# The second expert block's first product by seven block products (Strassen's 2x2 scheme), tokens in halves

## The chip, the core and the metric

The kernel runs on one core of a Trainium2 chip. A core has a matrix engine (TensorE, PE in the rows), a vector engine (VectorE, DVE), a scalar engine (ScalarE, ACT), a general engine (GpSimd, POOL) and a queue engine (SyncE, SP) that issues the transfers here. Each takes its own instructions in order and waits on semaphores for the others. TensorE reads SBUF and writes PSUM (eight banks of 128x512 float32); the others move results back to SBUF. The metric is the device time of one execution in microseconds (us), as a median of several.

## The reference, cut to what matters

```python
# attn_out: causal linear attention with decay, B=2, H=8, S=768, D=64 -> x of 1536 tokens x 512
# part one (1536 tokens, 512 -> 2048 -> 512)
h = x @ w_in
g = h * clip(h + 3, 0, 6) / 6
x = g @ w_out
# part two: 8 experts, each 512 -> 1024 -> 512, all tokens through all experts
logits = x @ w_gate;  P = exp(logits - logits.max())
for _ in range(8):
    P /= P.sum(1, keepdims=True) + 1e-9
    P /= P.sum(0, keepdims=True) + 1e-9
    P *= N / E
for e in range(8):
    h = maximum(x @ w1[e], 0)          # "first product"
    out += P[:, e:e+1] * (h @ w2[e])   # "second product"
```

The inputs w_in and w_out come as float64; everything else is float32.

## The kernel before

Every large product is made in three float32r matmuls of 128 rows: each operand is split into a rounded part hi and a rest lo, and hi x hi, hi x lo and lo x hi are summed in PSUM. ScalarE makes a hi (a copy), VectorE the lo behind it (a subtraction).

Attention takes the first 80 us or so. Then one list of steps, `steps`, runs: 48 steps of part one (three token blocks of 512, the 16 tiles of 128 hidden features in groups of 4, 6, 6), then 192 steps of part two (8 experts x 3 token blocks x 8 tiles of 128 hidden features). A step has a `stage_a` (12 matmuls at L312: one tile of the hidden h for 512 tokens, over 4 slices of the 512 inputs, in PSUM tag "s0") and a `stage_b` (12 matmuls at L348: what this tile adds to four accumulators of 128x512 in tags "s1" and "r"). `stage_a` of step s+2 is issued ahead of `stage_b` of step s (`LOOK` = 2), so that the hidden tile is evicted (L327 hi with ReLU, L328 lo) two steps before it is needed. `finish` takes the accumulators to `o` after the last tile of a group: L380 multiplies by the gate P and adds.

The weights of both parts come through one queue of loads and splits (`load_w`, `splitting`, L163 and L165 in part two), 13 slots deep, worked off by `pump` between steps. Each weight of part two is loaded once.

The gate hangs on the steps by a table, `put`: logits of a block as three times eight float32r matmuls (L407), transposes (L415), then from the third step of part two on one call of `gate_cols` a step: a small matmul (L453, tile gc) that sums columns over all tokens, and eight short VectorE instructions (L457 to L447) that normalise P by columns and by rows; the next call's matmul needs their result.

```python
    put(2 * (NSF + 3), gate_exp)
    for i in range(NITER):
        put(2 * (NSF + 4 + i), gate_cols, i == NITER - 1)
```

Of the kernel before, what the change touches and what calls it, by code (L numbers as in the profile page):

```python
# [18 lines left out]
P = 128  # L19
# [12 lines left out]
NLD = E * F2T  # L32
NW = 8
NX = 5
# [13 lines left out]
def kernel(  # L48
# [15 lines left out]

    ps_s = ctx.enter_context(tc.tile_pool(name="ps_s", bufs=2, space=PSUM))
    const = ctx.enter_context(tc.tile_pool(name="const", bufs=1))
    xp = ctx.enter_context(tc.tile_pool(name="xp", bufs=NBLK))
    wp = ctx.enter_context(tc.tile_pool(name="wp", bufs=NW))
    sk = ctx.enter_context(tc.tile_pool(name="sk", bufs=2))
    sp = ctx.enter_context(tc.tile_pool(name="sp", bufs=3))  # L70

    wg_raw = const.tile([P, KT, E], F32, name="wg_raw")
    lg = const.tile([P, NTT, E], F32, name="lg")
# [6 lines left out]
    wkeys = [("f", i) for i in range(F1T)] + [("e", i) for i in range(NLD)]  # L80
# [3 lines left out]
    raw_next = iter([u for u in units if u[0] == "f" or u[2] == 0])  # L84
    state_ = {"started": 0, "done": 0, "step": -1}

    def load_w():
        unit = next(raw_next, None)
        if unit is None:
            return  # L90
        kind, i, part = unit
        t = sp.tile([P, 2 * BLK], U32, tag="raw", name="raw")
        if kind == "f":
            nc.sync.dma_start(out=t, in_=wf_in[i, :, part * BLK:(part + 1) * BLK].bitcast(U32))
            raw_t[unit] = t
        else:
            nc.sync.dma_start(out=t, in_=we_in[i].bitcast(U32))
            for j in range(2):
                raw_t[kind, i, j] = t[:, j * BLK:(j + 1) * BLK]

    def slot_free():
        n = state_["started"] // 2
        if n < NW:
            return True
        if n < NW + NX:
            return "x" in pools
        return last_use[wkeys[n - NW - NX]] <= state_["step"]

    def splitting():
# [8 lines left out]
        for kind, i, part in units:  # L118
# [8 lines left out]
            if part == 0:  # L127
                pool = pools["x" if index[kind, i] % (NW + NX) >= NW else "w"]
                hi = pool.tile([P, 2 * BLK], F32R, tag="whi", name="whi")
                lo = pool.tile([P, 2 * BLK], F32R, tag="wlo", name="wlo")  # L130
                w_t[kind, i] = (hi, lo)
            r = slice(part * BLK, (part + 1) * BLK)
            if kind == "f":

                word = t.rearrange("p (n t) -> p n t", t=2)
                lw, hw = word[:, :, 0], word[:, :, 1]
                top = t.bitcast(U16).rearrange("p (n t) -> p n t", t=4)[:, :, 3]
                w = sp.tile([P, BLK], U32, tag="w", name="w", bufs=2)
                nc.vector.tensor_scalar(out=w, in0=lw, scalar1=29, scalar2=None, op0=ALU.logical_shift_right)  # L139
                yield True  # L140
                nc.vector.scalar_tensor_tensor(  # L141
                    out=w, in0=hw, scalar=0x80000000, in1=w, op0=ALU.bitwise_and, op1=ALU.bitwise_or
                )
                yield True
                nc.vector.tensor_scalar(out=top, in0=top, scalar1=0x7FFF, scalar2=None, op0=ALU.bitwise_and)  # L145
                nc.scalar.activation(out=top, in_=top, func=AF.Relu, bias=ebias, scale=1.0)  # L146
                yield True
                if tail:
                    low()
                    yield True  # L150
                nc.vector.scalar_tensor_tensor(  # L151
                    out=w, in0=hw, scalar=3, in1=w, op0=ALU.logical_shift_left, op1=ALU.bitwise_or
                )
                load_w()
                t = w.bitcast(F32)
                nc.scalar.activation(out=hi[:, r], in_=t, func=AF.Copy)
                tail.append((lo[:, r], t, hi[:, r]))
                yield True
            else:
                t = t.bitcast(F32)  # L160
                if tail:
                    low()
                nc.scalar.activation(out=hi[:, r], in_=t, func=AF.Copy)  # L163
                yield True
                nc.vector.tensor_tensor(out=lo[:, r], in0=t, in1=f32(hi[:, r]), op=ALU.subtract)  # L165
                if part:
                    load_w()
                state_["done"] += 1
                yield True
# [8 lines left out]
    def rate(s):  # L178

        most = 2  # L180
        for n, k in enumerate(wkeys):
            left = 2 * n + 2 - state_["done"]
            if left > 0 and first_use[k] <= s + 12:
                most = max(most, -(-left * (5 if k[0] == "f" else 2) // max(1, first_use[k] - LOOK - s)))
# [7 lines left out]
    x_t, x2_t = {}, {}  # L192

    def x_tiles(name):
        hi = xp.tile([P, KT, BLK], F32R, tag="xhi", name=name + "hi")
        lo = xp.tile([P, KT, BLK], F32R, tag="xlo", name=name + "lo")
# [3 lines left out]
    at = ctx.enter_context(ExitStack())  # L200
    at1 = at.enter_context(tc.tile_pool(name="at1", bufs=1))
    at2 = at.enter_context(tc.tile_pool(name="at2", bufs=2))
# [66 lines left out]
    def attend(n):  # L269
# [17 lines left out]
        if at_ == 0:  # L287
            x_t[bl] = x_tiles("x")
# [11 lines left out]
    steps += [("e", b, e * F2T + f, f, F2T, e) for e in range(E) for b in range(NBLK) for f in range(F2T)]  # L300
    g_t, acc_b, mo = {}, {}, {}

    def stage_a(s):
        kind, b, wi, f, nf, part = steps[s]
        whi, wlo = weights((kind, wi))
        xhi, xlo = (x_t if kind == "f" else x2_t)[b]
# [9 lines left out]
        if kind == "f":  # L316
            t = sp.tile([P, BLK], F32, tag="t", name="t", bufs=1)
            nc.scalar.activation(out=t, in_=h, func=AF.Relu, bias=three, scale=1.0)  # L318
            pump(1)
            nc.vector.scalar_tensor_tensor(  # L320
                out=t, in0=t, scalar=6.0, in1=h, op0=ALU.min, op1=ALU.mult
            )
            nc.scalar.activation(out=hi, in_=t, func=AF.Copy)  # L323
            pump(1)
            nc.vector.tensor_tensor(out=lo, in0=t, in1=f32(hi), op=ALU.subtract)  # L325
        else:
            nc.scalar.activation(out=hi, in_=h, func=AF.Relu)  # L327
            nc.vector.scalar_tensor_tensor(  # L328
                out=lo, in0=h, scalar=0.0, in1=f32(hi), op0=ALU.max, op1=ALU.subtract
            )  # L330
        g_t[s] = (hi, lo)

    def stage_b(s):
# [6 lines left out]
        for i in range(4):  # L340
            cs = slice(i * P, (i + 1) * P)
            ws = slice(BLK + i * P, BLK + (i + 1) * P)
            if kind == "f":
                ops = [(whi[:, ws], ghi), (whi[:, ws], glo), (wlo[:, ws], ghi)]
            else:
                ops = [(ghi[:, cs], whi[:, BLK:]), (ghi[:, cs], wlo[:, BLK:]), (glo[:, cs], whi[:, BLK:])]
            for j, (l, r) in enumerate(ops):
# [3 lines left out]
            if f == nf - 1:  # L351
                finish(kind, b, part, i)

    def finish(kind, b, part, i):
        o = mo["o"]
        tt = b * 4 + i
        if kind == "f" and part == 0:
            nc.scalar.activation(out=o[:, tt], in_=acc_b[i], func=AF.Copy)  # L358
# [267 lines left out]
```

## Time and profile before

| | |
|---|---|
| time, median of 3 runs | 1411.91 us (1411.49 to 1413.43) |
| the profiled execution: its time, its span in the trace | 1412.86 us, 1411.0 us |
| TensorE busy | 1390.6 us, 99% of the span |
| VectorE busy | 498.6 us, 35% |
| ScalarE busy | 341.1 us, 24% |
| transfers | 68.90 MB, 49 GB/s on average |

A matmul's own record overlaps the next one's, so the busy time of TensorE says that it was never without work, and not how long one matmul holds it: that is the distance from start to start. For VectorE and ScalarE the duration of a record is read as it stands; two that are independent of one another overlap a little.

### The profile page before, as it was taken

The page shows a single profiled execution, that of the slowest core. Times are in us where ns is not written, and L with a number is a line of the kernel's source. Part 1 is how long each engine was busy: PE and PEld are TensorE (multiplying, and loading weights), DVE is VectorE, ACT ScalarE, POOL GpSimd, SP SyncE. Part 2 cuts the span into 40 slices and gives each one's busy share as a digit, 9 for nine tenths or more (in the row PEclk, how much of TensorE's full clock was granted, in tenths as well). Part 3 has the DMA queues.
Part 4 walks back from the last instruction along what each step waited for, and adds up shares of the span by engine and source line. Part 5 has one row for each costly group of instructions (what it writes and reads, how often), then busy time and mean ns, then how long its engine had stood idle before and what let it go on. Part 6 is the DMA issues. An engine that isn't in the chain of part 4 may idle for free.

```text
span 1411.0 us, 14967 instructions
## 1 busy us (share of the span) xinstructions
PE 1390.6 (99%) x6379; PEld 1136.4 (81%) x6379; DVE 498.6 (35%) x820; ACT 341.1 (24%) x548; POOL 26.9 (2%) x26
## 2 busy tenths in 40 slices
PE   7899999999999999999999999999999999999998
PEld 6678788888888888888888888888888888888887
DVE  5876767554442321222123222222221232121211
ACT  3565545443211211111122111111121111111110
POOL 3300000000000000000000000000000000000000
PEclk9999999999999999999999999999999999999999
DMA  8622212121100110011011001200110011000000
GB/s 328 218 82 82 75 60 75 46 61 44 45 16 15 45 45 15 31 45 45 0 45 46 30 1 45 60 16 15 45 45 16 31 45 45 0 0 1 30 30 30
DMA packets 20370, 68.90 MB, mean 49 GB/s; under 512 B 2512, under 2 KB 2512, under 8 KB 20304
## 3 DMA queue, kind: packets, MB, share of 16 engines
q1 hardware_dynamic: 20304, 67.95, 14.7%
q8 instruction: 50, 0.82, 0.3%
q14 instruction: 16, 0.13, 0.0%
HBM read 64.79 MB, written 3.15 MB: 48 GB/s over the span
## 4 chain that ended last, share of the span: by engine, by line
PE 92%; DVE 4%; ACT 2%; DMA 1%; issue 1%; SPq 0%; ACTq 0%
PE acc L348 46%; PE h L312 45%; ACT raw L146 1%; DMA raw<-in_wf 1%; DVE w L151 1%; DVE raw L145 1%; DVE a L251 1%; DVE w L141 0%; PE l L407 0%; DVE w L139 0%; DVE xlo L292 0%; DVE t L320 0%; ACT t L318 0%; DVE glo L325 0%; ACT ghi L323 0%
## 5 line engine op out<-in xcount | busy, mean ns | idle before, releaser
L328 DVE SCALAR_TENSOR_TENSOR glo<-h,ghi 128x512 fp32r<-128x512 f32 x192 | 132.8, 692 | 751.9 <-ACT ghi L327 751.8
L327 ACT ACTIVATE ghi<-h 128x512 fp32r<-128x512 f32 x192 | 114.7, 597 | 866.7 <-PE h L312 866.7
L312 PE MATMUL h<-x2hi,whi 128*128 128x512 f32 x768 | 302.8, 394 | 0.0
L348 PE MATMUL acc<-whi,ghi 128*128 128x512 f32 x768 | 302.1, 393 | 0.0
L348 PE MATMUL acc<-wlo,ghi 128*128 128x512 f32 x768 | 302.1, 393 | 0.0
L312 PE MATMUL h<-x2hi,wlo 128*128 128x512 f32 x768 | 301.9, 393 | 0.0
L348 PE MATMUL acc<-whi,glo 128*128 128x512 f32 x768 | 301.6, 393 | 0.0
L312 PE MATMUL h<-x2lo,whi 128*128 128x512 f32 x768 | 300.1, 391 | 0.0
L348 PEld LDWEIGHTS acc<-whi,glo 128*128 128x128 f32 x768 | 144.7, 188 | 32.8
L348 PEld LDWEIGHTS acc<-wlo,ghi 128*128 128x128 f32 x768 | 144.7, 188 | 32.5
L312 PEld LDWEIGHTS h<-x2lo,whi 128*128 128x128 f32 x768 | 144.7, 188 | 32.5
L348 PEld LDWEIGHTS acc<-whi,ghi 128*128 128x128 f32 x768 | 144.3, 188 | 32.9
L312 PEld LDWEIGHTS h<-x2hi,wlo 128*128 128x128 f32 x768 | 144.2, 188 | 32.9
L312 PEld LDWEIGHTS h<-x2hi,whi 128*128 128x128 f32 x768 | 144.3, 188 | 31.1
L165 DVE TENSOR_TENSOR wlo<-raw,whi 128x512 fp32r<-128x512 f32 x128 | 87.4, 683 | 14.8 <-ACT whi L163 14.8
L163 ACT ACTIVATE whi<-raw 128x512 fp32r<-128x512 f32 x128 | 79.9, 624 | 15.2 <-PE acc L348 15.2
L312 PE MATMUL h<-xhi,whi 128*128 128x512 f32 x192 | 75.5, 393 | 0.8 <-DVE t L320 0.8
L348 PE MATMUL acc<-ghi,whi 128*128 128x512 f32 x192 | 75.6, 394 | 0.5 <-ACT o L358 0.5
L348 PE MATMUL acc<-ghi,wlo 128*128 128x512 f32 x192 | 75.6, 394 | 0.0
L348 PE MATMUL acc<-glo,whi 128*128 128x512 f32 x192 | 75.4, 393 | 0.0
L312 PE MATMUL h<-xhi,wlo 128*128 128x512 f32 x192 | 75.2, 392 | 0.0
L312 PE MATMUL h<-xlo,whi 128*128 128x512 f32 x192 | 75.2, 392 | 0.0
(83 smaller groups left out, 841.6 us busy)
## 6 DMA issues: line engine op xcount, KB each, us to landing
raw<-in_we SPq DMA_DIRECT2D x64, 512.0 KB, 3.5
raw<-in_wf SPq DMA_DIRECT2D x32, 512.0 KB, 3.6
qk<-in_qk SPq DMA_DIRECT2D x12, 512.0 KB, 5.0
kv<-in_kv SPq DMA_DIRECT2D x12, 512.0 KB, 5.8
out<-o SPq DMA_DIRECT2D x12, 256.0 KB, 2.1
tq<-in_tq SPq DMA_DIRECT2D x5, 256.0 KB, 5.4
dmask<-in_dmask SPq DMA_DIRECT2D x2, 256.0 KB, 4.1
gk<-in_gk SPq DMA_DIRECT2D x1, 24.0 KB, 7.0
```

Of the source, the lines that this page charges most:

```text
L145: nc.vector.tensor_scalar(out=top, in0=top, scalar1=0x7FFF, scalar2=None, op0=ALU.bitwise_and)
L146: nc.scalar.activation(out=top, in_=top, func=AF.Relu, bias=ebias, scale=1.0)
L151: nc.vector.scalar_tensor_tensor(out=w, in0=hw, scalar=3, in1=w, op0=ALU.logical_shift_left, op1=ALU.bitwise_or)
L163: nc.scalar.activation(out=hi[:, r], in_=t, func=AF.Copy)
L165: nc.vector.tensor_tensor(out=lo[:, r], in0=t, in1=f32(hi[:, r]), op=ALU.subtract)
L251: nc.vector.tensor_tensor(out=a, in0=t[j], in1=dmask[:, j], op=ALU.mult)
L312: nc.tensor.matmul(h, w[:, ks], x[:, k], start=(n == 0), stop=(n == 3 * KT - 1))
L327: nc.scalar.activation(out=hi, in_=h, func=AF.Relu)
L328: nc.vector.scalar_tensor_tensor(out=lo, in0=h, scalar=0.0, in1=f32(hi), op0=ALU.max, op1=ALU.subtract)
L348: nc.tensor.matmul(acc_b[i], l, r, start=(f == 0 and j == 0), stop=(f == nf - 1 and j == 2))
```

## The change

Part two is taken out of the step list. Tokens are handled in two halves of 768 (`NU` = 2, `UT` = 768), each half in two parts of 384 (`SB`). For one pair of hidden tiles (256 features; 32 pairs a half, 64 in all) the first product is a 2x2 block product: two halves of the 512 inputs, two hidden tiles, two token parts. Winograd's form of Strassen's scheme makes it in seven block products instead of eight. Each block product (`product`) is six matmuls of 384 columns: two input slices, three terms each. The sums of token blocks are made once a half (`x_forms`: four VectorE sums and seven splits of 128x768), the sums of weight blocks for every pair (`w1_forms`: four sums of 256 columns, splits of 512, 256, 512 and 512), and the products are put together in `pair` by five VectorE additions of 384 columns and two ScalarE copies, before four ReLU splits (`relu_parts`). The second product (`outputs`) keeps its matmuls of 512 columns, 36 a pair, and is spread between the block products of the next two pairs: an iteration `it` issues pairs 2it and 2it+1 and the second product of pairs 2it-2 and 2it-1. The first iteration has no second product to spread, and at the turn to the second half of the tokens (it = 16) the second product is issued in one piece ahead of the pairs, together with that half's `x_forms`. As each weight is used for either half, it is loaded and split twice. The gate's calls follow one another from the third slot of the first iteration on, one a slot (a slot is one block product), its logits as plain float32 matmuls of 32 output columns. In part one, `finish` writes the tiles y2 of 768 tokens, weights have 10 slots in place of 13, and in its last six steps the first `x_forms` and `w1_forms` are made. `stage_a`, `stage_b`, `finish` and `splitting` lose their branches for part two.

```diff
...
+    def parts(hi, lo, t):
+        nc.scalar.activation(out=hi, in_=t, func=AF.Copy)
+        nc.vector.tensor_tensor(out=lo, in0=t, in1=f32(hi), op=ALU.subtract)
+
+    def w1_forms(i):
+        r = raw1.pop(i)
...
+        parts(hi[:, A11:A12 + 1], lo[:, A11:A12 + 1], r[:, 0].rearrange("p (k c) -> p k c", k=2))
+        yield True
+        nc.vector.tensor_tensor(out=t[:, S1 - S1], in0=a21, in1=a22, op=ALU.add)
+        yield True
+        nc.vector.tensor_tensor(out=t[:, S3 - S1], in0=a11, in1=a21, op=ALU.subtract)
+        yield True
+        nc.vector.tensor_tensor(out=t[:, S2 - S1], in0=t[:, S1 - S1], in1=a11, op=ALU.subtract)
+        parts(hi[:, A22], lo[:, A22], a22)
+        yield True
+        nc.vector.tensor_tensor(out=t[:, S4 - S1], in0=a12, in1=t[:, S2 - S1], op=ALU.subtract)
+        load_pair(i + 2, 0)
+        yield True
+        for n in range(2):
+            parts(hi[:, S1 + 2 * n:S3 + 1 + 2 * n], lo[:, S1 + 2 * n:S3 + 1 + 2 * n], t[:, 2 * n:2 * n + 2])
+            yield True
...
+    def product(i, bank, w, x, start, stop):
+        whi, wlo = w1_t[i]
+        xhi, xlo = xf[x]
+        n = 0
+        for k in range(2):
+            ks = slice(k * P, (k + 1) * P)
+            for l, r in ((whi, xhi), (whi, xlo), (wlo, xhi)):
+                nc.tensor.matmul(
+                    bank[:, 0:SB], l[:, w, ks], r[:, k],
+                    start=(start and n == 0), stop=(stop and n == 5), skip_group_check=True,
+                )
+                n += 1
+
+    def relu_parts(i, f, j, t):
...
+        nc.scalar.activation(out=hi, in_=t, func=AF.Relu)
+        nc.vector.scalar_tensor_tensor(out=lo, in0=t, scalar=0.0, in1=f32(hi), op0=ALU.max, op1=ALU.subtract)
+        q_t[i, f, j] = (hi, lo)
+
+    def pair(i):
...
+        b1 = bank("s0")
+        product(i, b1, A11, B11, True, True)
+        yield
+        p1 = tmp("p1")
+        nc.scalar.activation(out=p1, in_=b1[:, 0:SB], func=AF.Copy)
+        b2 = bank("s0")
+        product(i, b2, S2, T2, True, True)
+        yield
+        u2 = tmp("u2")
+        add(u2, b2[:, 0:SB], p1)
+        b3 = bank("s1")
+        product(i, b3, S1, T1, True, True)
+        yield
+        p5 = tmp("p5")
+        nc.scalar.activation(out=p5, in_=b3[:, 0:SB], func=AF.Copy)
+        b4 = bank("r")
+        product(i, b4, S3, T3, True, True)
+        yield
+        u3 = tmp("u3")
+        add(u3, b4[:, 0:SB], u2)
+        product(i, b1, A12, B21, False, True)
+        yield
+        relu_parts(i, 0, 0, b1[:, 0:SB])
+        product(i, b3, S4, B22, False, True)
+        yield
+        add(p1, b3[:, 0:SB], u2)
+        add(p5, u3, p5)
+        relu_parts(i, 0, 1, p1)
+        product(i, b4, A22, T4, False, True)
+        yield
+        relu_parts(i, 1, 1, p5)
+        add(u3, b4[:, 0:SB], u2)
+        relu_parts(i, 1, 0, u3)
+        yield
+
+    def outputs(n):
...
+            acc = ps_s.tile([P, BLK], F32, tag="y", name="acc")
+            for f in range(4):
...
+                for k, (l, r) in enumerate(((ghi, whi), (ghi, wlo), (glo, whi))):
+                    nc.tensor.matmul(
+                        acc, l[:, cs], r[:, f % 2], start=(f == 0 and k == 0), stop=(f == 3 and k == 2)
+                    )
...
+        for it in range(NIT // 2 + 1):
+            outs = outputs(it - 1) if it else iter(())
+            chunks = 4 * TU if it else 0
...
+            if turn:
+                forming = x_forms(2 * it // NPR)
+                for n in range(chunks):
+                    next(outs)
+                    if n % 3 == 0:
+                        next(forming, None)
+                drain(forming)
+                chunks = 0
+            done = slot = 0
+            for n, i in enumerate(range(2 * it, min(2 * it + 2, NIT))):
+                job = itertools.chain(*jobs[n])
+                for _ in pair(i):
+                    slot += 1
+                    while done * 16 < chunks * slot:
+                        next(outs)
+                        done += 1
+                    for _ in range(2 if it else 1):
+                        next(job, None)
+                    if 2 < slot:
+                        fn = next(gate, None)
+                        if fn:
+                            fn()
+                drain(job)
+            drain(outs)
```

Three places show how instructions stand now. First, TensorE's list at one of the gate's small matmuls: before, in the first steps of part two.

```order
L348 MATMUL acc<-wlo,ghi 128x512
L348 MATMUL acc<-whi,glo 128x512
L453 MATMUL gc<-pm,ones 128x96
L312 MATMUL h<-x2hi,whi 128x512
L312 MATMUL h<-x2lo,whi 128x512
```

And after, in the second pair of the first iteration.

```order
L551 MATMUL h<-xl,w1hi 128x384
L551 MATMUL h<-xh,w1lo 128x384
L425 MATMUL gc<-pm,ones 128x96
L551 MATMUL h<-xh,w1hi 128x384
L551 MATMUL h<-xl,w1hi 128x384
```

Between two such small matmuls there stood 24 matmuls of 512 columns before; now there are the six of 384 columns of one block product.

Second, VectorE's list in that place (second pair of the first iteration): one turn of the gate's chain, what stands ahead of it and behind it. Here s and w1lo belong to the weight forms of the next pair, u_2929 and u_2883 to this pair's sums.

```order
L483 TENSOR_TENSOR s<-s,raw_2666 128x256
L467 TENSOR_TENSOR w1lo<-raw_2666,w1hi 128x256
L429 TENSOR_REDUCE c<-gc 128x8
L432 TENSOR_SCALAR c<-c 128x8
L435 RECIPROCAL c<-c 128x8
L436 TENSOR_TENSOR pm<-pm,c 128x96
L416 TENSOR_REDUCE r<-pm 128x12
L417 TENSOR_SCALAR r<-r 128x12
L418 RECIPROCAL r<-r 128x12
L419 TENSOR_TENSOR pm<-pm,r 128x96
L569 TENSOR_TENSOR u_2929<-h,u_2883 128x384
L486 TENSOR_TENSOR s<-raw_2666,s 128x256
```

Seven such turns stand in the first iteration, one between any two block products of its second pair; before, two instructions of the step stood between two turns, and a turn fell on every step.

Third, VectorE's list within one pair of a middle iteration (o is the eviction of the second product, gl the ReLU split, p and u the sums of block products).

```order
L467 TENSOR_TENSOR w1lo<-raw_4219,w1hi 128x256
L569 TENSOR_TENSOR u_4481<-h,p_4465 128x384
L640 SCALAR_TENSOR_TENSOR o<-acc,pm,o 128x512
L486 TENSOR_TENSOR s<-raw_4219,s 128x256
L467 TENSOR_TENSOR w1lo<-s,w1hi 128x512 x2
L467 TENSOR_TENSOR w2lo<-raw_4258,w2hi 128x512
L569 TENSOR_TENSOR u_4521<-h,u_4481 128x384
L640 SCALAR_TENSOR_TENSOR o<-acc,pm,o 128x512
L467 TENSOR_TENSOR w2lo<-raw_4258,w2hi 128x512
L562 SCALAR_TENSOR_TENSOR gl<-h,gh 128x384
```

A pair has 22 VectorE instructions: five of 512 columns for weight splits, three of 512 for evictions, nine of 384 and five of 256. Before, a step had one of 512 for the hidden tile, and evictions and weight splits in bursts.

## Rows read from the trace of the kernel before

**Rows 1.** The page's first part: busy time and share of the span, instructions.

```profile
PE 1390.6 (99%) x6379; PEld 1136.4 (81%) x6379; DVE 498.6 (35%) x820; ACT 341.1 (24%) x548; POOL 26.9 (2%) x26
```

**Rows 2.** The page's chain that ended last, by engine and by line.

```profile
PE 92%; DVE 4%; ACT 2%; DMA 1%; issue 1%; SPq 0%; ACTq 0%
PE acc L348 46%; PE h L312 45%; ACT raw L146 1%; DMA raw<-in_wf 1%; DVE w L151 1%; DVE raw L145 1%; DVE a L251 1%; DVE w L141 0%; PE l L407 0%; DVE w L139 0%; DVE xlo L292 0%; DVE t L320 0%; ACT t L318 0%; DVE glo L325 0%; ACT ghi L323 0%
```

**Rows 3.** Windows: part one's end, and part two (busy us and records of each engine).

```profile
core 0: us, PE busy (x) PEld busy (x) DVE busy (x) ACT busy (x) POOL busy (x), PEclk, DMA share, GB/s
200.00:320.00 120.00, 120.00 (x524) 97.58 (x523) 73.56 (x121) 56.49 (x85) 0.50 (x2) 1.00 0.21 66
800.00:1000.00 200.00, 200.00 (x869) 163.22 (x868) 48.19 (x73) 32.67 (x57) 0.00 (x0) 1.00 0.09 27
```

**Rows 4.** Groups by line and form: TensorE's matmuls of part two.

```profile
L312 PE MATMUL h<-x2hi,whi 128*128 128x512 f32 x768 | 302.8, 394 | 0.0
L348 PE MATMUL acc<-whi,ghi 128*128 128x512 f32 x768 | 302.1, 393 | 0.0
```

**Rows 5.** Timelines of TensorE and of its weight loads (PEld) around one gc.

```profile
370.65 0.35 PE L453 MATMUL gc<-pm,ones 128*128 128x96 f32 x2
370.79 0.48 PE L312 MATMUL h<-x2hi,whi 128*128 128x512 f32 x1
371.11 0.39 PE L312 MATMUL h<-x2lo,whi 128*128 128x512 f32 x1
...
370.76 0.19 PEld L312 LDWEIGHTS h<-x2hi,whi 128*128 128x128 f32 x1
370.88 0.19 PEld L312 LDWEIGHTS h<-x2lo,whi 128*128 128x128 f32 x1
```

**Rows 6.** Groups by line and form: VectorE, long and short instructions.

```profile
L165 DVE TENSOR_TENSOR wlo<-raw,whi 128x512 fp32r<-128x512 f32 x128 | 87.4, 683 | 14.8 <-ACT whi L163 14.8
L380 DVE SCALAR_TENSOR_TENSOR o<-acc,pm,o 128x512 f32<-128x512 f32 x84 | 57.2, 743 | 4.9 <-PE acc L348 4.9
L378 DVE TENSOR_SCALAR o<-acc,pm 128x512 f32<-128x512 f32 x8 | 5.4, 745 | 0.0
L447 DVE TENSOR_TENSOR pm<-pm,r 128x96 f32<-128x96 f32 x8 | 2.1, 258 | 0.3
```

**Rows 7.** Timeline of VectorE: four evictions in a row.

```profile
437.46 2.72 DVE L378 TENSOR_SCALAR o<-acc,pm 128x512 f32<-128x512 f32 x4
```

**Rows 8.** Timeline of VectorE: one turn of the gate's chain.

```profile
405.50 0.26 DVE L457 TENSOR_REDUCE c<-gc 128x8 f32<-128x96 f32 x1 [1.66 <-PE gc L453]
...
407.28 0.26 DVE L447 TENSOR_TENSOR pm<-pm,r 128x96 f32<-128x96 f32 x1
```

**Rows 9.** Groups by line and form: ScalarE, a long and a short one.

```profile
L163 ACT ACTIVATE whi<-raw 128x512 fp32r<-128x512 f32 x128 | 79.9, 624 | 15.2 <-PE acc L348 15.2
L439 ACT ACTIVATE pm<-lg,nm 128x96 f32<-128x96 f32 x1 | 0.4, 376 | 2.2 <-DVE nm L438 2.2
```

**Rows 10.** Timeline of TensorE in attention: plain float32 matmuls, full and half width.

```profile
23.56 1.06 PE L261 MATMUL r<-kv,ks 128*128 128x128 f32 x8
...
25.63 1.09 PE L276 MATMUL y<-a,kv 128*64 128x128 f32 x16
```

**Rows 11.** Groups: the gate's work on TensorE.

```profile
L407 PE MATMUL l<-x2lo,wg 128*128 128x512 f32 x12 | 4.8, 396 | 0.0
L453 PE MATMUL gc<-pm,ones 128*128 128x96 f32 x16 | 2.8, 258 | 0.0
L415 PE MATMUL lt<-ones,l 16*128 16x16 f32 x12 | 1.3, 214 | 0.0
```

**Rows 12.** Windows in attention: TensorE's busy time and its granted clock (PEclk).

```profile
8.00:11.45 3.45, 1.62 (x26) 1.50 (x28) 0.42 (x1) 0.00 (x0) 1.04 (x1) 1.00 1.04 411
11.45:14.87 3.42, 3.42 (x24) 2.87 (x20) 1.16 (x3) 0.97 (x2) 0.29 (x1) 0.50 1.03 407
43.10:46.50 3.40, 1.78 (x24) 1.28 (x22) 2.30 (x3) 1.50 (x4) 1.75 (x2) 1.00 1.00 359
```

**Rows 13.** The page's issues of transfers: part two's weights.

```profile
raw<-in_we SPq DMA_DIRECT2D x64, 512.0 KB, 3.5
```

More of the change, by code (lines that the diff above doesn't have):

```diff
@@ L92, in load_w @@
         t = sp.tile([P, 2 * BLK], U32, tag="raw", name="raw")
[L93 to L99, printed above, removed]
+        nc.sync.dma_start(out=t, in_=wf_in[i, :, part * BLK:(part + 1) * BLK].bitcast(U32))
+        raw_t[unit] = t
+    LATE = F1T - GROUPS[-1]
     def slot_free():
@@ L299 @@
         steps += [("f", b, f0 + f, f, n, g) for b in range(NBLK) for f in range(n)]
-    steps += [("e", b, e * F2T + f, f, F2T, e) for e in range(E) for b in range(NBLK) for f in range(F2T)]
-    g_t, acc_b, mo = {}, {}, {}
+    g_t, acc_b, mo, y2 = {}, {}, {}, {}
     def stage_a(s):
@@ L402, in logits @@
-    def logits(b):
-        t = ps_s.tile([P, BLK], F32, tag="y", name="l")
-        n = 0
-        for k in range(KT):
-            for x in x2_t[b]:
-                nc.tensor.matmul(t, mo["wg"][:, k], x[:, k], start=(n == 0), stop=(n == 2 * KT - 1))
-                n += 1
-        mo["l"] = l = sp.tile([P, BLK], F32, tag="t", name="l", bufs=1)
-        nc.scalar.activation(out=l[0:2 * E], in_=t[0:2 * E], func=AF.Copy)
-    def logits_to_rows(b):
-        t = ps_s.tile([P, 4, 2 * E], F32, tag="y", name="lt")
-        for i in range(4):
+                finish(b, part, i)
@@ L493, with drain @@
+    def drain(it):
+        for _ in it:
+            pass
     last_use, first_use = {}, {}
@@ new lines @@
+        for i in range(2):
+            load_pair(i, 1)
+        gate = [lambda n=n, f=f: f(n) for n in (2, 3) for f in (logits, logits_to_rows)]
+        gate += [gate_max, gate_max2, gate_exp]
+        gate += [lambda i=i: gate_cols(i == NITER - 1) for i in range(NITER)]
+        gate = iter(gate)
+        for it in range(NIT // 2 + 1):
+            outs = outputs(it - 1) if it else iter(())
+            chunks = 4 * TU if it else 0
+            jobs = []
+            for i in (2 * it, 2 * it + 1):
+                if i < NIT:
+                    jobs.append([w1_forms(i + 1)] if i + 1 < NIT else [])
+                    jobs[-1].append(w2_parts(i))
+            turn = it and (2 * it) % NPR == 0 and 2 * it < NIT
+            if turn:
[3 more added lines that the diff above has]
+                    if n % 3 == 0:
+                        next(forming, None)
+                drain(forming)
+                chunks = 0
[15 more added lines that the diff above has]
+            drain(outs)
+            for i in (2 * it - 2, 2 * it - 1):
+                w2_t.pop(i, None)
```

426 lines of the change are left out of this document (256 added, 170 removed).

## The prediction

> **What bounds the kernel now.** The page's first part comes first: TensorE has a record running for 99% of the span, VectorE for 35% [rows 1]. The chain of waits says that this is no coincidence: 92% of the path to the end is TensorE, and nearly all of that the two matmul lines of the steps [rows 2]. The windows then show where: from 200 us on TensorE never idles, at full granted clock, with VectorE busy for 48 of 200 us in part two [rows 3]. So the time of part two is its number of matmuls times their distance, and other engines count only where they keep TensorE waiting.
>
> The distance is not the 394 ns of a record, which overlaps its neighbour [rows 4]. 869 records in 200 us are one per 0.2302 us [rows 3]. Each product of part two has three groups of 768 such matmuls, of which one stands for either in [rows 4]: 2304 of them, 2304 x 0.2302 = 530.4 us for each product.
>
> **The first product: 2304 matmuls of 512 columns become 2688 of 384.** (64 pairs x 7 block products x 6.) The columns fall by an eighth, the number grows by a sixth, so all hangs on what one of 384 costs, which no row shows. Bounds: if all of 0.2302 us goes with the columns, 0.75 x 0.2302 = 0.1727 us. If only the streaming does, one column a cycle at the 2.4 GHz that the full granted clock is, then 128 columns less save 0.0533 us: 0.1769 us. I take 0.1745, near the middle, as nothing in the rows favours either. 2688 x 0.1745 = 469.1 us, **-61.3 us** (-66.2 to -54.9).
>
> The Trainium skill (TensorE: Matmul & The Clock Gate, "Back-to-back issue gap") puts the distance at the columns over 2.4 GHz plus about 2.5 ns. That would be 216 ns for 512 columns where the windows give 230 [rows 3], so the trace disagrees; for 384 columns it would be 162.5 ns, and this term -93.6 us by it.
>
> Can the weight load, which must run ahead of every matmul, be the limit? Behind a gc, whose own matmuls are too short to hide loads, two float32r loads of 128x128 start 0.12 us apart (370.76, 370.88), and the next only with the matmul at 371.11 [rows 5]. So a load needs about 0.12 us and lies beside 0.1745.
>
> **The second product** keeps 2304 matmuls of 512 columns: 0 us.
>
> **Does VectorE keep up in a middle iteration?** A pair has 42 matmuls of 384 columns and 36 of 512: 7.33 + 8.29 = 15.6 us of TensorE. VectorE's sizes are new; I draw a line through 258 ns for 96 columns and 683 for 512 [rows 6]: 421 ns for 256, 552 for 384, 945 for 768. A pair has five weight splits of 512 (3.42), three evictions of 743 ns (2.23) [rows 6], five sums or splits of 256 (2.10), and nine of 384 (4.97): 12.7 us. Records overlap a little: four evictions in a row take 2.72 us [rows 7], 0.68 each against 0.745 [rows 6], so 0.065 less for each of 22 behind another: 11.3 us. It fits with 2.9 to 4.3 us to spare. The order gives the waits room as well: TensorE adds to b1, b3 and b4 again two slots (about 4 us) after VectorE or ScalarE could read them, and the two banks of acc are turned over every 5 us. ScalarE has 12 instructions a pair, at 624 ns for 512 columns and less for 384 [rows 9] some 7 us. I put small waits at **+2 us** over the 60 interleaved pairs (0 to +18).
>
> Weights are loaded twice: two transfers of 512 KB a pair, which land in 3.5 us [rows 13], for 15.6 us of work, issued two pairs ahead. The six output transfers at the turn stand ahead of loads in SP's queue, but those loads are for two pairs later. Hidden: 0. Part one's last six steps take on 11 instructions of 768 columns (10.4 us), eight of `w1_forms` (4.2 us) and their own work (some 8 us) on VectorE, within 33 us of matmuls; VectorE was busy 74 of 120 us there [rows 3]. Hidden: 0, but for the wait named below.
>
> **The first iteration** has no second product to cover it, and the gate in it. TensorE has 84 matmuls, 14.7 us. VectorE, with sizes as above less the overlap: its first pair has six instructions of 512 (3.7), five of 256 (1.8), nine of 384 (4.4) and four short ones of the gate (0.9), 10.8 us. Some 1.5 to 2 us come on top, since three of the four gl stand right behind the ScalarE instruction that they need (about 0.55 us for 384 columns between the two sizes of [rows 9]), so 13.0. Its second pair has 9.3 us of the same, the part around the exponential (1.2 us) and seven turns of the chain. A turn takes 2.04 us from the first instruction's start to the last one's end [rows 8]: 14.3 us. That is 24.8 us. Between two turns goes the round to TensorE's gc and back, about 0.65 us, mostly behind the 0.9 us of other VectorE work that stands there. With 3.5 us for what isn't covered and for splits behind ScalarE, 28.3. TensorE is tied to it: each gc stands ahead of the next block product and waits for the turn before. The block product (1.05 us) runs while the next turn does, and then TensorE waits. So the iteration takes 13.0 + 28.3 = 41.3 us where its matmuls take 14.7: **+26.6 us** (+15, if waits are nil and the gate's instructions slip under the first pair, to +33).
>
> **The turn to the second half.** The second product in one piece is 72 matmuls, 16.6 us, and covers `x_forms` (11 x 0.88 = 9.7 us) and six evictions (4.1). Pairs 32 and 33 then run without cover: VectorE has 9.3 us a pair and about 1.6 behind ScalarE, 10.9, twice 21.8 us, against 14.7: **+7.1 us** (+3 to +12).
>
> **The gate outside that iteration.** Before, it cost TensorE 24 logits matmuls (5.5 us), eight gc that push the next matmul back by 0.23 us each (370.65 to 371.11 is two distances [rows 5]), 1.8 us, and 12 transposes [rows 11] of about 0.1 us: 8.5 us. Now two of the four logits stand in part one. A plain float32 record of 128 columns takes about 0.11 us at full width (8 in 0.9 us), and 16 records of half width took no longer than 8 of full width [rows 10]: different column groups of the array ran side by side. Four of 384 columns on 32 output columns each are then 0.7 us (2.7 if not side by side). With six transposes (1.3), one gc (0.2) and one wait of 1.6 us, where the first logits need the last of eight half-size additions of `finish` just issued, that is 4.5 us: **-4.0 us** (-4 to 0).
>
> **The sum** is made against the profiled execution: its span of 1411.0 us, with 1.9 us around it; it is 1.0 us above the median, and only differences are carried over. -61.3 + 2 + 26.6 + 7.1 - 4.0 = -29.6. From 1411.9: 1382.3, **1382 us**.
>
> **Rivals.**
> *VectorE becomes the bound in the middle (slower).* If records don't overlap (12.7 us) and seven hand-overs between VectorE and ScalarE in a pair cost 0.6 us each, it needs 16.9 us a pair against 15.6. 60 pairs x 1.3 = +78 in place of +2, 1458 us. It turns slower than before above 16.1 us a pair. For: the gl at a pair's end come in a chain, sum, ScalarE, VectorE, three times. Against: 4 us of room, and hand-overs cover one another when two splits are under way.
> *The weight load is the bound (slower).* Then 384 columns cost what 512 do: 2688 x 0.2302 = 618.8, 150 us more than I put in, 1532 us. The change loses from 0.1855 us a matmul on. The two starts 0.12 us apart speak against it.
> *A cheap opening.* If the gate's instructions slip into waits that VectorE has anyway, the first iteration costs 12 us less: 1370 us.
> *Small waits.* 0.3 us in each interleaved pair, as each block product now carries a wait of its own where a step had few: +18 in place of +2, 1398 us.
> *No cost beyond streaming.* If the 17 ns that 512 columns take beyond 213 went away for shorter matmuls, 384 would take 0.160 us: -39 more, 1343 us. Against: every matmul of 512 columns in the windows carries that cost. By the rule of the Trainium skill cited above it would be 1350.
> *The clock falls in the first iteration.* TensorE would have work there for little over a third of the time. In attention the clock stayed at 2.4 GHz with 1.78 of 3.40 us busy, but after 1.62 of 3.45 us busy came a stretch at 1.2 GHz [rows 12]. A block product would take 2.1 us and still fit beside a turn of the chain; with the stretch behind it that costs about 4 us, 1386, which is within the likeliest case.
>
> **How the numbers follow.** Likeliest, 56%: the sum as it stands, 1374 to 1392, with or without the clock. Cheap opening 17%, small waits 12%, VectorE the bound 7%, load the bound 4%, streaming only 4%. The range 1366 to 1402 takes in the first three (85%), and the bounds of 384 columns (-5 to +6). A measurement here can tell about 0.2% (2.8 us) from no change. Faster: the 89% of the cases below 1409, less 2 for a mix of small and large waits, 87%; slower 11%; same 2%.
>
> **What the profile after would show.** Starts 0.17 to 0.177 us apart within a block product (the first term); 15.6 to 16 us a pair in the middle with VectorE busy for some 75 to 80% (the second); about 41 us from the first matmul of L551 to the first of L627 (the third), and there gc waiting for VectorE and the chain of waits going over L416 to L436; pairs 32 and 33 in about 22 us. If the distance in a block product is 0.2 us or more, or a middle pair takes over 16.1 us, the prediction is wrong.

## The result: faster than predicted, 1365.8 us

The changed kernel takes **1365.79 us** (median of 4 runs, 1364.82 to 1366.78) against 1411.95 of the kernel before: a ratio of 0.967 (95% interval 0.9655 to 0.9688). The prediction was 1382 with a range of 1366 to 1402, so the sign was right and the time lies 0.2 us under the range. The profiled execution took 1364.82 us, with a span of 1363.0. That is 48.0 us less than the span of before, where the sum said 29.6. (The medians differ by 46.2: the profiled execution of before lies 0.9 us above its median, this one 1.0 below.)

The page of the kernel after, its busy times and its chain of waits (they answer to [rows 1, 2]):

```profile
PE 1331.2 (98%) x6771; PEld 1173.1 (86%) x6771; DVE 963.7 (71%) x1830; ACT 551.5 (40%) x1003; POOL 28.0 (2%) x28
...
PE 88%; DVE 6%; ACT 3%; DMA 1%; issue 1%; SPq 0%; ACTq 0%
```

TensorE still sets the time, and VectorE has twice the work. By windows: the opening (first L551, the block products, to first L627, the second product), 30 middle pairs, the second product in one piece, pairs 32 and 33, 30 middle pairs, the last piece. The number behind each busy time counts records, also those that began ahead of the window.

```profile
335.70:374.80 39.10, 28.88 (x130) 23.69 (x130) 31.46 (x97) 12.26 (x27) 0.00 (x0) 0.75 0.22 73
374.80:840.60 465.80, 465.79 (x2338) 421.30 (x2338) 341.78 (x672) 185.54 (x366) 0.00 (x0) 1.00 0.21 69
840.60:857.00 16.40, 16.40 (x74) 13.42 (x73) 13.65 (x17) 6.15 (x9) 0.00 (x0) 1.00 0.21 80
857.00:877.70 20.70, 17.87 (x92) 16.91 (x91) 19.41 (x39) 10.67 (x23) 0.00 (x0) 0.92 0.34 115
877.70:1342.60 464.90, 464.90 (x2335) 420.77 (x2334) 338.08 (x652) 182.10 (x357) 0.00 (x0) 1.00 0.19 63
1342.60:1358.90 16.30, 16.30 (x73) 13.33 (x71) 4.72 (x7) 0.00 (x0) 0.00 (x0) 1.00 0.22 81
```

In the two middle stretches TensorE never idles. In the opening it works 28.88 of 39.10 us at a mean granted clock of 0.75, with VectorE busy for 31.46. A timeline of TensorE shows the distances (first column: start) inside one block product and one chunk of the second product:

```profile
502.28 0.39 PE L627 MATMUL acc<-w2hi,gh 128*128 128x512 f32 x1
502.51 0.39 PE L627 MATMUL acc<-w2lo,gh 128*128 128x512 f32 x1
502.74 0.40 PE L627 MATMUL acc<-w2hi,gl 128*128 128x512 f32 x1
502.97 0.34 PE L551 MATMUL h<-xh,w1hi 128*128 128x384 f32 x1
503.15 0.34 PE L551 MATMUL h<-xl,w1hi 128*128 128x384 f32 x1
503.32 0.34 PE L551 MATMUL h<-xh,w1lo 128*128 128x384 f32 x1
503.50 0.33 PE L551 MATMUL h<-xh,w1hi 128*128 128x384 f32 x1
```

Matmuls of 384 columns start 0.174 us apart, as the sum had it (0.1745). Those of 512 start 0.227 apart, and 0.235 at a change to 384. Before, the mean was 0.2302 [rows 3]. VectorE's new sizes came out as the line through two old ones gave them (predicted 552, 421 and 945 ns), in groups by line and form:

```profile
L569 DVE TENSOR_TENSOR u<-h,u 128x384 f32<-128x384 f32 x128 | 70.4, 550 | 1.0 <-PE h L551 1.0
...
L479 DVE TENSOR_TENSOR s<-raw 128x256 f32<-128x256 f32 x64 | 26.7, 417 | 0.0
...
L467 DVE TENSOR_TENSOR xl<-s,xh 128x768 fp32r<-128x768 f32 x8 | 7.6, 955 | 1.3 <-ACT xh L466 1.2
```

TensorE's waits (us in total, times, longest) show what the opening waits for above all: the normalisation chain (L419 ends a turn).

```profile
PE gc L425 <- DVE pm L419: 7.3, 6, 3.5
...
PE gt L401 <- DVE m L396: 2.3, 1, 2.3
PE h L551 <- DVE u L569: 2.2, 2, 1.6
```

### The profile page after: what moved, and what is told of

Its sections match the earlier page's. It is cut to its first block, busy times and chain, and to the rows that moved or that the text cites. A ratio compares the mean times of both kernels' runs of the same rounds, so it can differ in the third digit from the quotient of the medians.

```text
span 1363.0 us, 17381 instructions
## 1 busy us (share of the span) xinstructions
PE 1331.2 (98%) x6771; PEld 1173.1 (86%) x6771; DVE 963.7 (71%) x1830; ACT 551.5 (40%) x1003; POOL 28.0 (2%) x28
## 4 chain that ended last, share of the span: by engine, by line
PE 88%; DVE 6%; ACT 3%; DMA 1%; issue 1%; SPq 0%; ACTq 0%
PE acc L627 39%; PE h L551 33%; PE acc L346 8%; PE h L319 8%; ACT raw L162 1%; DMA raw<-in_wf 1%; DVE w L167 1%; DVE raw L161 1%; DVE a L259 1%; DVE w L155 0%; DVE w L157 0%; DVE w1lo L467 0%; DVE t L326 0%; DVE xlo L300 0%; DVE gl L562 0%
## 5 line engine op out<-in xcount | busy, mean ns | idle before, releaser
L551 PE MATMUL h<-xh,w1hi 128*128 128x384 f32 x896 | 304.7, 340 | 2.8 <-DVE u L569 2.2
L551 PE MATMUL h<-xh,w1lo 128*128 128x384 f32 x896 | 303.5, 339 | 0.0
L551 PE MATMUL h<-xl,w1hi 128*128 128x384 f32 x896 | 303.1, 338 | 0.0
L627 PE MATMUL acc<-w2hi,gl 128*128 128x512 f32 x768 | 301.7, 393 | 0.0
L627 PE MATMUL acc<-w2hi,gh 128*128 128x512 f32 x768 | 299.9, 391 | 0.0
L627 PE MATMUL acc<-w2lo,gh 128*128 128x512 f32 x768 | 298.9, 389 | 0.0
L551 PEld LDWEIGHTS h<-xh,w1hi 128*128 128x128 f32 x896 | 170.4, 190 | 21.4 <-DVE u L569 2.9
L551 PEld LDWEIGHTS h<-xl,w1hi 128*128 128x128 f32 x896 | 170.3, 190 | 19.5
L627 PEld LDWEIGHTS acc<-w2hi,gl 128*128 128x128 f32 x768 | 144.2, 188 | 30.9
L551 PEld LDWEIGHTS h<-xh,w1lo 128*128 128x128 f32 x896 | 170.1, 190 | 0.0
L627 PEld LDWEIGHTS acc<-w2lo,gh 128*128 128x128 f32 x768 | 144.4, 188 | 13.5
L627 PEld LDWEIGHTS acc<-w2hi,gh 128*128 128x128 f32 x768 | 144.0, 188 | 13.8 <-DVE o L640 0.2
L326 DVE SCALAR_TENSOR_TENSOR t<-t,h 128x512 f32<-128x512 f32 x48 | 33.1, 689 | 66.1 <-ACT t L324 65.9
```

What stands on the lines that cost most here:

```text
L326: nc.vector.scalar_tensor_tensor(out=t, in0=t, scalar=6.0, in1=h, op0=ALU.min, op1=ALU.mult)
L551: nc.tensor.matmul(bank[:, 0:SB], l[:, w, ks], r[:, k], start=(start and n == 0), stop=(stop and n == 5), skip_group_check=True,)
L627: nc.tensor.matmul(acc, l[:, cs], r[:, f % 2], start=(f == 0 and k == 0), stop=(f == 3 and k == 2))
```

## The experiments

Two questions stood open: what sets the distance of matmuls of 512 columns, for which the prediction had used one mean, and which of the change's parts gave or cost what.

**The place of tiles in SBUF, kernel before.** In the trace of before the distance goes from 224 to 241 ns, and two thirds of the distances return within 1 ns a group of eight tiles (192 matmuls) later. Set beside the byte addresses that the compiled program gives the tiles, it shows that a matmul and the next one are nearer to one another where the moving operand of the first (what streams through) and the weights of the next begin at the same address modulo 256 bytes. The edit moves all tiles behind a small pool by 128 bytes (the new tile has two buffers of 64):

```diff
+    pad = sk.tile([P, 16], F32, tag="pad", name="pad")
...
+        nc.vector.memset(pad, 0.0)
```

> The kernel before with 128 bytes of padding a partition, nothing else: it moves the weight slots of the second pool, the hidden tiles and o, so that the moving operand of every large matmul and the weights loaded while it streams start at addresses equal modulo 256 bytes. Before, that held for 2772 of 5770 neighbours in the program; in its trace those lie 228.1 ns apart and the others 232.7. Theory one (the place in SBUF sets the distance): all at about 227.5 to 228, 2998 x 4.7 ns = 14 us less, 1396 to 1400 us. Rival (the distance of 227 ns in the changed kernel comes from the mixture with short matmuls or from what other engines do at the time): no change, 1411 to 1413 us.

Measured: 1390.82 us, ratio 0.9845 (0.9832 to 0.9859), 21.6 us faster by unused bytes, and not only the 14 expected: the neighbours that had begun alike before, too, went from 228 ns to 227. Windows of the padded kernel, in the stretches of [rows 3]:

```profile
200.00:320.00 120.00, 120.00 (x534) 98.90 (x533) 73.76 (x122) 55.83 (x84) 0.50 (x2) 1.00 0.20 62
800.00:1000.00 200.00, 200.00 (x884) 165.62 (x883) 52.57 (x80) 34.83 (x61) 0.00 (x0) 1.00 0.09 29
```

884 records in 200 us in place of 869. Counted by starts it is 882 in place of 867, 0.2267 us each in place of 0.2305. So the 0.2302 of the prediction belonged to the placement of before, and not to the matmul; and it was read 0.3 ns short, since two of the 869 records had begun ahead of the window.

**The same for the changed kernel**, 32 bytes on the left side of SBUF (part one's tokens, the token and weight forms of part two), which gives all operands the same start modulo 256 bytes:

```diff
+    pad = const.tile([P, 8], F32, name="pad")
...
+        nc.vector.memset(pad, 0.0)
```

> The changed kernel with 32 bytes of padding ahead of its left pools, so that in part one the first two token blocks, and the step from the second product to a block product, start at equal addresses modulo 256 too (6130 of 6146 neighbours in place of 4905). Theory one (place in SBUF): the 418 steps seen at 235 ns (448 in the program) and some 400 of part one at 233 fall to 227, 448 x 7.8 ns + 400 x 6.2 ns = 6 us less, 1358 to 1361 us. Rival (mixture): no change, 1365 to 1367 us.

Measured: 1375.02 us (0.9735, 0.9721 to 0.9748), 9 us slower than without the pad, where 6 us less were expected. Windows in part one and in the middle, of the padded kernel:

```profile
200.00:300.00 100.00, 100.00 (x443) 82.81 (x442) 53.86 (x90) 38.27 (x53) 0.00 (x0) 1.00 0.12 37
400.00:800.00 400.00, 400.00 (x1985) 359.44 (x1984) 291.09 (x564) 156.55 (x307) 0.00 (x0) 1.00 0.20 68
```

and of the changed kernel as it is:

```profile
200.00:300.00 100.00, 100.00 (x437) 81.76 (x436) 52.91 (x90) 37.69 (x51) 0.00 (x0) 1.00 0.11 37
400.00:800.00 400.00, 400.00 (x2010) 362.13 (x2009) 293.52 (x570) 158.97 (x312) 0.00 (x0) 1.00 0.20 68
```

Part one gained as expected, and the middle lost 25 matmuls in 400 us. The timeline of the padded kernel, where the second product in one piece begins, tells why equal addresses don't suffice:

```profile
844.88 0.33 PE L552 MATMUL h<-xh,w1lo 128*128 128x384 f32 x1
845.05 0.39 PE L628 MATMUL acc<-w2hi,gh 128*128 128x512 f32 x1
845.28 0.40 PE L628 MATMUL acc<-w2lo,gh 128*128 128x512 f32 x1
845.52 0.40 PE L628 MATMUL acc<-w2hi,gl 128*128 128x512 f32 x1
845.75 0.39 PE L628 MATMUL acc<-w2hi,gh 128*128 128x512 f32 x1
...
847.59 0.39 PE L628 MATMUL acc<-w2hi,gl 128*128 128x512 f32 x1
847.82 0.39 PE L628 MATMUL acc<-w2hi,gh 128*128 128x512 f32 x1
848.04 0.39 PE L628 MATMUL acc<-w2lo,gh 128*128 128x512 f32 x1
848.27 0.39 PE L628 MATMUL acc<-w2hi,gl 128*128 128x512 f32 x1
```

Behind the change of size the distances go 229, 233, 236, 224, 231, 236, 228, 233, 231 ns, and then 226, 227, 227 for as long as the piece lasts, with nothing changed in line, tiles or sizes. There is a rhythm that can be lost, and that takes about nine matmuls to come back here. In the middle the size changes seven times a pair, every three to nine matmuls, and in this kernel the rhythm of 512 columns is not back before the next change. It is lost among the 384 columns: in the two places where the 512 columns ahead of a change had the rhythm, the change itself cost nothing (226 and 227 ns), but the six of 384 behind it stood 171 to 185 ns apart.

**Only the second product's weights moved**, by a tile of two small buffers ahead of them, so that w2 and gh begin 64 bytes apart (here w2 is what streams, and gh is loaded as TensorE's weights):

```diff
+        if i == 0:
+            pad = pools["m2"].tile([P, 4], F32, tag="pad", name="pad")
+            nc.vector.memset(pad, 0.0)
```

> The changed kernel with 32 bytes of padding ahead of the second product's weights, so that these and the hidden tiles no longer start at equal addresses modulo 256 (64 bytes apart). Theory one (place in SBUF): the 1856 distances within the second product go from 227 ns to 232 to 235, +9 to +15 us, 1375 to 1381 us. Rival (mixture with short matmuls): no change, 1365 to 1367 us.

Measured: 1369.35 us (0.9697, 0.9683 to 0.971; the lowest run 1369.03), 3.6 us slower than the changed kernel, whose highest run is 1366.78: the direction was right, the size a third of what was expected, since the rule was still the wrong one (a price for each pair, and no memory of the pairs ahead).

**The rule, put to a test.** Over the traces of the two kernels and of all eight experiments, with starts from the addresses in the compiled programs, take each matmul of 512 columns in the large products that follows three distances of 226 or 227 ns. If its moving operand and the next weights begin at the same address modulo 256 bytes, the next distance is 227 or less 15,631 of 15,636 times (12 more, of over half a microsecond, are left out as waits); if the weights begin 32, 128 or 224 bytes further (224 is 32 the other way), it is 228 or more 1,803 of 1,803 times. Of these 1,803, however, 1,433 are also a change to 384 columns; the places alone stand behind 370, at 32 and 128 bytes. (In the last four traces, taken after the rule stood, it is 5,115 of 5,116 and 1,012 of 1,012.) In the changed kernel two of part one's three token blocks began 32 bytes off their weights. The next kernel puts them right and leaves part two as it was; it starts from the version with the later gate (below).

```diff
+    pad = const.tile([P, 8], F32, name="pad")
...
                 pools["xf"] = pool("xf", "left", bufs=1, reuse_waits="tile")
+                gap = pools["xf"].tile([P, 56], F32, tag="gap", name="gap")
```

> The version with the later gate (1351.2 us), with every tile on the left side of SBUF 32 bytes further, and then the tiles of part two's token forms and weight forms moved back to where they lay modulo 256 bytes. What changes for TensorE is thus only the place of part one's token operands: two of three blocks began at 192 modulo 256 where the weights begin at 224; now all begin at 224. Theory (from the traces so far: a matmul of 512 columns that follows others at 226 to 227 ns keeps that rhythm, 10516 of 10520 times, if its moving operand and the next weights begin at the same address modulo 256 bytes, and loses it, 791 of 791 times, if they don't): the first products of part one fall from 232 to about 227 ns, part two stays as it is, in all 2.6 us less: 1348 to 1349.5 us. Rival (the distance goes with something else that the earlier pads moved): part two's second product goes from 227 to about 230 again, as when all of the left side lay 32 bytes further: 1357 us or more.

Measured: **1348.27 us** (0.9549, 0.9535 to 0.9563), 2.9 less than that version. The interval overlaps that version's, but the windows agree with the theory: 442 records in the 100 us of part one in place of 437, and the middle undisturbed, 2013 as in the version with the later gate (last row).

```profile
200.00:300.00 100.00, 100.00 (x442) 82.82 (x442) 52.08 (x87) 36.84 (x50) 0.00 (x0) 1.00 0.10 32
400.00:800.00 400.00, 400.00 (x2013) 362.18 (x2012) 299.79 (x595) 156.64 (x308) 0.00 (x0) 1.00 0.20 68
...
400.00:800.00 400.00, 400.00 (x2013) 362.22 (x2012) 301.69 (x597) 158.53 (x311) 0.00 (x0) 1.00 0.20 69
```

The same with a gap of 32 elements in place of 56 puts part two's forms 128 bytes off:

> The same, but part two's token forms and weight forms begin 128 bytes away from the second product's tiles modulo 256 bytes in place of 32. It asks why a change from 512 to 384 columns costs 8.3 ns in every run so far, at an equal start as at one 32 bytes off. If the start addresses decide there too, then the distance at the change moves, up or down, and with it those of the matmuls behind it: at 32 bytes they were undisturbed, at 0 bytes the second product went to 230.7. If the change of size costs 8.3 ns whatever the place, only what follows it moves. Theory: 128 bytes off is as bad as equal or worse: 1354 to 1362 us against 1348 to 1349.5 of the version 32 bytes off. Rival: no difference, 1348 to 1350 us.

Measured: 1355.78 us (0.9603, 0.9587 to 0.9619), 7.5 us slower than with 32 bytes. The change from 512 to 384 columns then costs 5.8 ns more than the rhythm in place of 8.3, but the 384 columns behind it are disturbed (177.8 ns on average in place of 174.2). The place decides there too. The 8.3 ns that the expectation took for equal starts as well were not the price of the change: in the kernel with 32 bytes the third matmul of 512 columns is followed 235.8 ns later, whether a change comes there or not, and where a change came in the rhythm it cost nothing.

```profile
400.00:800.00 400.00, 400.00 (x1994) 363.18 (x1994) 297.99 (x591) 156.08 (x307) 0.00 (x0) 1.00 0.20 68
```

**Eight block products in place of seven**, all else kept (no sums of blocks):

```diff
-        product(i, b2, S2, T2, True, True)
+        product(i, b2, A11, B12, True, False)
...
+        product(i, b2, A12, B22, False, True)
```

> The changed kernel with eight block products a pair in place of seven: no sums of token, weight or product blocks; halves, gate and interleaving kept. Theory one (the gain is that of the arithmetic: 384 matmuls of 384 columns less in all): the middle pairs take 1.04 us more, 16.56; 64 x 6 x 0.1737 = 66.7 us in all, less some 6 us at the turn and some 9 us in the opening, where VectorE, which loses about 5 us of work a pair, set the pace: about 1418 us (1412 to 1428), no faster than before. Rival (the gain came from the new order of work, the halves and the interleaving, and the seven products give little): under 1395 us.

Measured: 1421.11 us (1.0064, 1.0049 to 1.0079), slower than before, within the expected range. The operands of neighbours begin as far apart modulo 256 bytes as in the changed kernel, and an iteration in the middle takes 33.17 us in place of 31.07, two block products more. Theory one holds: the seven products with their sums are worth 55.3 us, and all else that the change brings costs 9 us. VectorE is down to 165 of 400 us in the middle, and the opening takes 34.0 us, pairs 32 and 33 18.0:

```profile
338.00:372.00 34.00, 28.27 (x143) 23.55 (x142) 23.53 (x81) 10.46 (x21) 0.00 (x0) 0.86 0.28 93
400.00:800.00 400.00, 400.00 (x2028) 364.38 (x2027) 164.86 (x270) 98.10 (x194) 0.00 (x0) 1.00 0.20 64
885.50:903.50 18.00, 18.00 (x105) 17.93 (x104) 9.87 (x18) 6.47 (x14) 0.00 (x0) 1.00 0.41 132
```

**More work for VectorE**, in each pair eight additions whose results are not used:

```diff
+            for _ in range(4):
+                nc.vector.tensor_tensor(out=z, in0=r[:, 0, 0:BLK // 2], in1=r[:, 1, 0:BLK // 2], op=ALU.add)
```

> The changed kernel with eight more VectorE additions of 256 columns in each pair, whose results nothing uses: about 2.9 us of VectorE a pair (eight times 0.42 less the overlap). Theory (VectorE keeps TensorE waiting only in the opening and in pairs 32 and 33, and has 4.2 of 15.5 us left elsewhere): 0 in the 60 middle pairs, 2 to 3 us in each of the four others: 1372 to 1379 us. Rival (VectorE is near its limit in the middle, as its hand-overs with ScalarE come on top of its busy time): at least 0.5 us in each middle pair as well, 1402 us or more.

Measured: 1379.55 us (0.9767, 0.9753 to 0.9782), 13.8 more than the changed kernel, half a microsecond above the expected range.

```profile
338.40:380.90 42.50, 29.13 (x130) 23.87 (x129) 34.72 (x105) 12.26 (x27) 0.00 (x0) 0.72 0.20 66
...
867.30:893.40 26.10, 19.72 (x93) 18.67 (x92) 24.38 (x53) 10.19 (x22) 0.00 (x0) 0.87 0.23 75
893.40:1356.00 462.60, 462.60 (x2325) 418.80 (x2324) 429.16 (x891) 175.75 (x357) 0.00 (x0) 1.00 0.19 64
```

The opening is 3.4 us longer and pairs 32 and 33 5.3; the pairs from 893.40 on take no more time, with VectorE busy 93% of the time (the window ends some ten matmuls ahead of that of the changed kernel; by starts the two agree within 0.1 us). The first 30 middle pairs took 2.8 us more, nearly all in two waits for VectorE (TensorE starts again at 394.7 and 457.9 us), and the piece between the halves 1.5 more. (In this profiled execution part one also begins 2.6 us later, where the edit changes nothing.) So VectorE, once it has caught up, is no bound in the middle, and it is where nothing covers it.

**The gate's chain moved behind the opening.** Logits on every second slot of the first iteration, and the eight turns (one gc and its VectorE instructions) on two slots of each pair of iterations 1 and 2, beside the second product, with the gc in the PSUM tags s1 and s0:

```diff
-                    if 2 < slot:
+                    if not it and slot > 2 and slot % 2:
...
+                    if it and slot % 8 in (2, 6):
+                        fn = next(cols, None)
+                        if fn:
+                            fn("s1" if slot % 8 == 2 else "s0")
```

> The changed kernel with the gate spread out: logits, maximum and exponential on every second slot of the first iteration, the eight calls of gate_cols on two slots of each pair of the second and third iteration, with accumulators of their own. Theory one (the gate's chain on VectorE, tied to the block products by TensorE's order, makes the opening long): the 39 us up to the first matmul of the second product shrink to 25 to 28, the clock falls less or not at all, the second and third iteration gain 0 to 3 us: 1352 to 1357 us. Rival (the opening is bound by VectorE's weight forms and splits, and the gate hides behind them): 36 to 39 us stay, 1362 to 1366 us.

Measured: 1351.2 us (0.9564, 0.9551 to 0.9577), 14.6 less than the changed kernel. The opening falls from 39.1 to 20.1 us (the first L627 starts at 356.38), at full clock, where 25 to 28 were expected; and the two iterations behind it give 5.5 back, since TensorE now waits there for the splits of the second product's weights (2.1 us for the first w2hi) and the clock falls once:

```profile
336.30:356.60 20.30, 19.55 (x117) 16.82 (x116) 17.24 (x39) 9.78 (x21) 0.00 (x0) 1.00 0.40 136
356.60:375.00 18.40, 16.08 (x73) 14.04 (x72) 14.20 (x41) 7.73 (x17) 0.00 (x0) 0.91 0.23 77
...
PE acc L627 <- ACT w2hi L466: 2.1, 1, 2.1
```

How much of the 19 us is the chain's own and how much the clock that fell beside it, this run doesn't separate.

With the tokens of part one moved it is the version of 1348.27 us, faster than both kernels.

## Why the prediction was right in sign and too high

By its own terms, in spans. The mark for the opening and the turn is the first L627, so either holds one more block product than the two pairs (1.05 us are added to the predicted 41.3 and 21.8, and taken from the middle). Differences are taken before rounding.

| stretch | predicted | measured | difference |
|---|---|---|---|
| opening | 42.3 | 39.1 | -3.3 |
| 60 middle pairs, waits included | 936.9 | 930.7 | -6.2 |
| pairs 32 and 33 | 22.8 | 20.7 | -2.2 |
| second product in one piece, twice | 33.1 | 32.7 | -0.4 |
| part two of before (2 x 530.4, one logits, eight gc) | 1064.8 | 1067.0 | -2.2 (more to gain) |
| part one with its logits | 0 | -2.6 | -2.6 |
| attention | 0 | -1.5 | -1.5 |

Together 18.4 us, the distance of -48.0 from -29.6; 1.9 of it is where the two profiled executions lie among their runs. One assumption failed, that the distance of 512 columns carries over; the other differences are sizes, all to the same side, and the range's low end allowed for less. Part two of before had more to gain because its matmuls stood 0.2305 us apart, not 0.2302 (1.4 of the 2.2 us).

**The first product: right in number, partly by luck.** 0.174 us a matmul was predicted at 0.1745, and undoing the seven products alone costs 55.3 us. In the rhythm 512 columns take 226.7 ns and 384 take 173.3, and either is the columns and 32 more at 2.4 GHz. The 53.3 ns between them are 128 columns at that clock: the upper bound, by which only the streaming gets shorter, had the mechanism. It came out at 0.1769 because it started from 0.2302, which the placement of before had made 3.5 ns longer than the rhythm. The middle of the bounds, taken for want of a reason for either, took 2.4 ns of that off again. The rule of the Trainium skill (TensorE: Matmul & The Clock Gate, "Back-to-back issue gap"), 2.5 ns over the columns, which it gives for the isolated gap, would be 162.5; the trace disagrees here too.

**The second product at 0 us: the step that failed.** "Keeps 2304 matmuls of 512 columns: 0 us" carried 0.2302 us over as if it came with the matmul. It came with the tiles' places, which the change moved: 29 of a pair's 36 now stand 227.1 ns apart, seven 235.0, the mean 228.6, or 1.6 ns less for 2160 of them, 3.4 us. Without these the time would be 1369, inside the range; of the 18.4 us they are the part whose cause the prediction left out. It was luck that they went down: 32 bytes cost 9 us, and before, 128 bytes were worth 21.6. The distances of 224 to 241 ns stood in the trace of before; the prediction averaged them.

**Small waits at +2: none.** VectorE is idle for 27% of a middle pair (20 to 25 were expected), a pair takes 15.53 us, at the low edge of the 15.6 to 16 forecast, and 2.9 us more work a pair cost the last 30 pairs nothing. VectorE is the bound only where the second product doesn't cover the pairs.

**The opening: right cause, too long.** The first pair took 12.5 us (predicted 13.0), the second 24.5 (28.3): the 3.5 us put on for what wasn't covered were too many. The gate's turns set the pace, as the wait of gc for pm and the gain of 14.6 us without them show. The clock fell there to 1.2 GHz as the rival had it, from 348.0 to 354.9 us and from 361.7 to 375.4, and most of the slower block products lay beside the chain.

**The turn: right cause, too long.** VectorE was busy for 19.4 of 20.7 us; its work behind ScalarE probably overlapped more than was allowed for, which no run tests. The clock fell here too, from 873.7 to 877.1 us, which the prediction didn't have: in the kernels with 32 bytes and with the shifted weights it didn't fall, and the same stretch took 19.3 us.

**The gate outside: a wait that wasn't there.** The first logits need tokens 0 to 383 only, which `finish` writes early; no wait stands ahead of them. That is 1.6 of part one's 2.6 us. Another 0.8 is again the distance, 229.6 ns in place of 230.4 over 1148 matmuls. The 1.5 us of attention are not explained: the start of part one differs by up to 2.9 us between the profiled executions here.

## What to carry to other kernels

A mean distance of matmuls is a property of one placement of tiles: before it is carried to a changed kernel, look at single starts, and if they vary with a pattern, move a pad of 32 or 128 bytes and measure, with the old kernel too. Fewer products at the price of more VectorE work pay where other matmuls cover that work; look for the stretches without cover (a first iteration, a turn), and keep serial chains of small instructions out of them. In a comparison, part of a gain can be placement, or placement can hide it: the change as it stands is 46 us faster than the kernel before, and 25 faster than the kernel before with 128 unused bytes.

## What the runs showed of the hardware

- TensorE's float32r matmuls, each with new weights of 128x128, have a rhythm of columns + 32 at 2.4 GHz (226.7 ns for 512, 173.3 for 384). Those of 512 columns kept it while the moving operand and the next weights began at the same address modulo 256 bytes, and each time that the weights began 32, 128 or 224 bytes further the next start came later. At equal starts a lost rhythm took some nine matmuls of 224 to 236 ns to return (the kernel with 32 bytes).
- A change from 512 to 384 columns cost 8.3 ns at starts 32 bytes apart and 5.8 at 128. At equal starts, seen twice behind the rhythm, it cost nothing, but the 384 columns behind it stood 171 to 185 ns apart.
- The change from 384 to 512 columns kept the rhythm (173.3 ns) where the weights loaded for the 512 columns (gh) began 32 bytes further than the moving operand of the 384 columns; at equal starts the 512 columns behind it began with 229, 233 and 236 ns. Why the 32 bytes help is open. That VectorE's accesses disturb the rhythm is unlikely: the distances of the second product are the same, within 0.3 ns, with VectorE idle and busy (226.9 and 227.1).
- At the clock's lower level matmuls of 384 columns stood 320 ns apart, which is the columns at 1.2 GHz with nothing added.
